# The quads' stages of a fused attention and mixture-of-experts kernel: behind a part's sums instead of between its products and its sums

## The chip, the cores and the metric

The kernel runs on one core of a Trainium2 chip. The metric is the device time of one execution in microseconds. The kernel before took 918.22 us, the median of three runs (918.18 to 922.17).

## The reference

For each of 4 batches, q, k and v have 3648 rows of 256 columns. The attention is over columns: q and k are normalised along the rows, a 256 x 256 matrix of their products goes through a softmax, and v is multiplied by it. The 14592 resulting rows x are then routed to 16 experts (4 groups of 4), each with two weight matrices:

```
s = kn.T @ qn / tau;  a = softmax(s);  x = v @ a
group = argmax(x @ w_group);  expert = argmax(x @ w_expert[group])
h = relu(x @ w1[group, expert])          # 256 -> 1024
out = gate weights * (h @ w2[group, expert])   # 1024 -> 256
```

## The kernel before

**Order of the whole.** The first third computes the attention, routes every row and scatters the rows into a buffer sorted by expert. Then the experts' work runs in three grains: 28 *items* of 512 rows of one expert each, 6 *quads* (128 rows, four pieces of 32 rows, each piece of an expert of its own), and up to 20 blocks of 128 rows behind the last item. The change touches the loop over the items, into which the quads are woven. From there on the program order on all five engines is written by hand.

**An item.** The loop runs over `seq`, 28 items times 8 parts (`f` = 0 to 7). One turn `n` does, for item `i` and part `f`:

- `ffn1(items[i], f)` (line 947): the part's *products*. Six matmuls of 512 columns give 128 of the 1024 hidden columns, in float32r pieces: w1 high with x high, w1 high with x low, w1 low with x high. ScalarE writes the high part of the Relu (`hh`, line 956), VectorE the low part (`hl`, line 957).
- The preparation of the next item: at f = 0 and 2 a half of its w1 is split into a high and a low part (lines 743 and 744, ScalarE and VectorE), at f = 5 and 6 a half of w2; at f = 3 and 4 its rows are turned and split.
- `ffn2(..., f - 2)` (lines 976 and 977): the *sums* of the part two turns back (`lag = 2`). For each of four groups of 128 rows, one matmul of 512 columns (`hh` with w2 high and low side by side) and one of 256 columns (`hl` with w2 high) add into that group's accumulator.
- After the sums of part 7, `finish` (line 1019): four times ScalarE scales one half of an accumulator into `ys` (line 993), VectorE adds the other half (line 994), and POOL scatters the rows (line 1005). `finish` of an item falls into part 1 of the next.

The four accumulators are four PSUM tiles (tags `acw` and `acc`, line 970), two of each, and each item takes all four. The products' outputs rotate over three PSUM tiles (tag `mm`), which the stages below share.

**A quad stage.** The quads' work is cut into 14 stages. The list `at` (line 1207) says in which of the last 24 items (j = i - 4) a stage stands: j = 0, 1, 3, 5, 7, ... 21, 22, 23. A stage does half of the hidden columns of one quad (`q_ffn1`, line 1091: 128 x 32 weights, 512 columns, four column tiles side by side) and half of the sums of the quad before (`q_ffn2`, line 1104, 256 columns). The first stage pair does only the former, the last only the latter. The stage's matmuls run at f = 2; its Relu goes to ScalarE (line 1094). VectorE transposes: the new quad's rows in 16 instructions (line 1076, `q_xT`), eight at f = 7 of the item before and eight at f = 0, for j = 0, 3, 7, 11, 15 and 19, where a quad begins; and the hidden rows at f = 3 to 6 (`q_hT`). `q_put` scales and scatters a finished quad at f = 3.

**Loads.** SP issues the weight loads and the 16 small copies that turn an item's rows (line 710). The quads' weights come through lines 1068 and 1071 into a single large tile (`qraw`, for one of the four pieces), two smaller ones (`qw`) and a ring (`qr`).

Of the kernel before, what the change touches and what calls it, by code (L numbers as in the profile page):

```python
# [61 lines left out]
def attention_moe(ctx: ExitStack, tc, q, k, v, tau, w_group, w_expert, w1, w2, out):  # L62
# [21 lines left out]
    def ring(*shape, name):  # L84
        return rp.tile([P, *shape], F32, tag="ring", name=name, bufs=RING)
# [602 lines left out]
    def fetch_x(d, tb, i):  # L688

        if d is items[0]:  # L690
            d["xg"] = raw_tile()[:, 0:4 * RW].rearrange("p (t w) -> p t w", t=4)
        else:
            d["xg"] = ring(4, RW, name="xg")
        d["nv"] = tb[1][:, i:i + 1]
        if tb is not tb_pre:
            gather(d["xg"].rearrange("p t w -> p (t w)"), tb[2][:, i:i + 1], 4)
            pause()
            return
        s = SP.value_load(tb[0][0:1, i, 1:2], min_val=0, max_val=DUMMY)
        ins = SP.dma_start(d["xg"].bitcast(I32), xs_d[ds(s, BIG), :].rearrange("(p t) w -> p t w", t=4))  # L700
        early.append(ins.ins)
        for o in late:
            tc.declare_no_dep(ins.ins, o, reason="the first items' slots have been filled")

    def quads_of(d):

        d["xq"] = ring(16, C // 4, name="xq")
        for q in range(4):
            for s in range(4):
                SP.dma_start(d["xq"][q * 32:(q + 1) * 32, s::4, :],  # L710
                             d["xg"][s * 32:(s + 1) * 32, :, q * 64:(q + 1) * 64])
# [160 lines left out]
    def where(i):  # L872
        return (items[i], tb_pre, i) if i < KPRE else (items[i], tb_big, i - KPRE)
# [114 lines left out]
    def put(d, t, src, on):  # L988
        ys = d["ys"]
        wcol = d["wc"][:, t:t + 1]  # L990
        if len(d["acc"]) == 4:
            a = d["acc"][t]
            ACT.activation(ys[:, t, :], a[:, 1, :], AF.Copy, scale=wcol)
            DVE.scalar_tensor_tensor(ys[:, t, :], a[:, 0, :], wcol, ys[:, t, :], ALU.mult, ALU.add)  # L994
        elif on == 0:
            ACT.activation(ys[:, t, :], src, AF.Copy, scale=wcol)
        else:
            DVE.tensor_scalar(ys[:, t, :], src, wcol, None, ALU.mult)
        if any(d is o for o in items[0:2]):
            held.append((d, t))  # L1000
        else:
            send(d, t)
# [16 lines left out]
    def finish(d):  # L1019
        d["ys"] = ring(4, C, name="ys")  # L1020
        for t in range(4):
            put(d, t, None if len(d["acc"]) == 4 else d["acc"][t // 2][:, t % 2, :], t // 2 if "xT" in d else 0)

    def fetch_big(i, which):
        d, tb, k = where(i)
        fetch_w(d, tb, k, which)
# [16 lines left out]
    def q_rows(q):  # L1043
        gather(qs["xg"][q % 2], tb_pc[2][:, q:q + 1], 1)
        pause()

    def q_stage(s):

        q, hf = divmod(s, 2)
        return ([(0, q, hf)] if q < NQ else []) + ([(1, q - 1, hf)] if q else [])  # L1050

    def q_weights(s, ps_):

        fetched = qs.setdefault(s, {})
        for p in ps_:
            w = wp.tile([P, 2048], F32, tag="wraw2", name="qraw", bufs=1) if p == 0 else None
            for second, q, hf in q_stage(s):
                e = SP.value_load(tb_pc[0][0:1, 4 * q + p, 0:1], min_val=0, max_val=E - 1)
                if p == 0:
                    t = w[:, second * 1024:(second + 1) * 1024]  # L1060
                elif p == 1:
                    t = rp.tile([P, 1024], F32, tag="L", name="qw", bufs=2)
                else:
                    t = ring(1024, name="qr")
                fs = slice(hf * 512, (hf + 1) * 512)
                if second:
                    fetched[1, p] = t = t.rearrange("p (f d) -> p f d", d=C)
                    SP.dma_start(t, w2e[ds(e, 1), fs, :].rearrange("o (c p) f -> p (o c) f", p=P))
                else:
                    fetched[0, p] = t = t.rearrange("p (c f) -> p c f", c=2)  # L1070
                    SP.dma_start(t, w1e[ds(e, 1), :, fs].rearrange("o (c p) f -> p (o c) f", p=P))
# [133 lines left out]
    host = lambda i: i - UN0 if 0 <= i - UN0 < 4 * NQ else None  # L1205
    LAST = 4 * NQ
    at = [0] + [2 * s - 1 for s in range(1, 2 * NQ)] + [LAST - 2, LAST - 1]
    stage = lambda j: at.index(j) if j in at else None
# [9 lines left out]
    seq = [(i, f) for i in range(NBIG) for f in range(8)]  # L1218
# [35 lines left out]
    for n in range(len(seq) + lag):  # L1254
        if n == 8 * KPRE:
            pt_.close()
            wide.append(ctx.enter_context(tc.tile_pool(name="pw", bufs=2, space=PSUM)))
        if n < len(seq):
            i, f = seq[n]
            j, jn = host(i), host(i + 1)  # L1260
            if f == 3:
                if KPRE < i + 2 < NBIG:
                    fetch_x(*where(i + 2))
            if jn is not None and f == 5 and i + 2 < NBIG:
                fetch_big(i + 2, "w1")
            for now_, to in ((j, plan), (jn, plan_n)):
                for s_, p_ in to.get((now_, f), ()):
                    q_weights(s_, p_)
            if f == 7 and KPRE < i + 2 < NBIG:
                quads_of(items[i + 2])  # L1270
            if j is not None and f == 1 and i + 1 < NBIG:
                fetch_big(i + 1, "w2")
            if first(j) is not None and f == 1:
                q = first(j)
                tokens(qs["ids"][q % 2], qs["xg"][q % 2][:, C:C + 1], slotq, tb_pc[1][:, q:q + 1])
            if i == NBIG - 1 and f == 4:
                POOL.drain()
                ns = nc.values_load(nsub[0:1, 0:1], min_val=0, max_val=NSUB)
                tc.mark_branch_hint_location("subs", engines=[ET.PE, ET.Pool, ET.DVE, ET.Activation, ET.SP])
            if first(jn) is not None and f == (1 if jn else 3):  # L1280
                q_rows(first(jn))
            ffn1(items[i], f)
            for h in side.get(n, ((), ()))[0]:
                h()
            if KPRE < i + 1 < NBIG:
                if f in (0, 2):
                    split_w(i + 1, "w1", f // 2)
                if f == 3:
                    turn_x(items[i + 1])
                if f == 4:  # L1290
                    split_x(items[i + 1])
                if f in (5, 6):
                    split_w(i + 1, "w2", f - 5)
            for q, a in ((jn, 0),) if f == 7 else ((j, 2),) if f == 0 else ():
                if first(q) is not None:
                    q_xT(first(q), a)
                    q_xT(first(q), a + 1)
            if j is not None:
                s_ = stage(j)
                for second, q, hf in q_stage(s_) if s_ is not None else ():  # L1300
                    if f == 2:
                        (q_ffn2 if second else q_ffn1)(s_)
                    if 3 <= f < 7 and not second:
                        q_hT(q, hf, f - 3)
                    if f == 3 and second and hf:
                        q_put(q)
        if lag <= n < len(seq):
            i, f = seq[n - lag]
            if i < NBIG - 1 or f < 8 - TAIL:
                ffn2(items[i], f)  # L1310
            if f == 7:
                finish(items[i])
        if n == len(seq) + lag - 2:
            sub_tiles()
        if n == len(seq) + lag - 1:

            d = items[NBIG - 1]
            d["ys"] = ring(4, C, name="ys")
            order = [(t, f) for t in range(4) for f in range(8 - TAIL, 8)]
            order.insert(TAIL, order.pop(TAIL - 1))  # L1320
            for t, f in order:
                sums(d, t, f)
                if f < 7:
                    continue
                a, w = d["acc"][t], d["wc"][:, t:t + 1]
                ACT.activation(d["ys"][:, t, :], a[:, 0, :], AF.Copy, scale=w)
                send(d, t)
        for h in side.get(n, ((), ()))[1]:
            h()
        scatter(NJ)  # L1330
        if n == 8 * (KPRE + 4):
            rgens.append(tables_sub())
        if n >= 8 * KPRE:
            advance(1)
# [85 lines left out]
```

## Time and profile before

| | before |
|---|---|
| median of three runs | 918.22 us |
| profiled execution | 924.53 us |
| its span | 922.6 us |
| TensorE busy (share of the span) | 907.9 us (98%) |
| VectorE, ScalarE, POOL busy | 716.1, 497.2, 390.0 us |
| granted TensorE clock, mean | 0.999 |
| DMA | 232 GB/s mean, 213.88 MB |

The busy time is that of one profiled execution, whose own time lies outside the range of the three runs. A busy TensorE is not TensorE at its peak: matmuls are pipelined and overlap in the timeline, so what it spends on one is read from start to start.

### The profile page before, as it was taken

Reading aid. Unit: us, or ns where it says so; the run is one execution under the profiler, and the core shown is the slowest. Engines: PE = TensorE matmul, PEld = TensorE weight load, DVE = VectorE, ACT = ScalarE, POOL = GpSimd, SP = SyncE. Lnnn points to the kernel's source line nnn. Section 1 sums busy time; section 2 is a strip of 40 time slices with the busy share of each in tenths; the row PEclk is TensorE's granted clock in tenths of the full one; section 3 lists DMA queues with packets and bytes.
Section 4 is the critical chain, followed back from the end, with each engine's and each line's share of the span. In section 5 each row is a group of like instructions: output and inputs, shape, how many; then the busy total and the mean of one; then the engine's idle time right before and its main releaser. Section 6 shows DMA issues by size and latency. Waiting matters only on the chain. (4 is left out here: it accounts for less than half of the span.)

```text
span 922.6 us, 16837 instructions
## 1 busy us (share of the span) xinstructions
PE 907.9 (98%) x5500; PEld 769.7 (83%) x5500; DVE 716.1 (78%) x1519; ACT 497.2 (54%) x831; POOL 390.0 (42%) x569
## 2 busy tenths in 40 slices
PE   9999999998999999999999999999999999999997
PEld 7899998998889987878787887878687878787887
DVE  6898998976999778878877767786677858785852
ACT  6789788676654445444545454445454444444432
POOL 0001887886588682322332334333433334323213
PEclk9999999999999999999999999999999999999999
DMA  9985868364854477777777777777776767777740
GB/s 301 359 290 187 310 226 297 129 212 163 297 168 155 146 270 249 251 244 248 254 248 246 248 251 256 251 236 234 241 229 222 246 225 229 229 239 247 244 159 36
DMA packets 159164, 213.88 MB, mean 232 GB/s; under 512 B 63107, under 2 KB 117643, under 8 KB 159072
## 3 DMA queue, kind: packets, MB, share of 16 engines
q1 hardware_dynamic: 144128, 168.23, 56.2%
q0 software_dynamic: 14944, 44.54, 12.9%
q8 instruction: 44, 0.72, 0.3%
q14 instruction: 48, 0.39, 0.1%
HBM read 170.33 MB, written 31.39 MB: 219 GB/s over the span
## 5 line engine op out<-in xcount | busy, mean ns | idle before, releaser
L947 PE MATMUL hmm<-xth,ww 128*128 128x512 f32 x888 | 314.7, 395 | 0.8 <-issue 0.8
L956 ACT ACTIVATE hh<-hmm 128x512 fp32r<-128x512 f32 x222 | 132.8, 599 | 333.6 <-PE hmm L947 306.9
L1005 POOL DMA_INDIRECT out<-ys,ids x112 | 126.0, 1125 | 365.8 <-DVE ys L994 338.8
L976 PE MATMUL wacc<-ww,hh 128*128 128x512 f32 x736 | 265.8, 394 | 0.0
L957 DVE SCALAR_TENSOR_TENSOR hl<-hmm,hh 128x512 fp32r<-128x512 f32 x222 | 152.2, 689 | 115.9 <-ACT hh L956 95.9
L977 PE MATMUL wacc<-ww,hl 128*128 128x256 f32 x736 | 206.4, 280 | 0.1
L947 PEld LDWEIGHTS hmm<-xth,ww 128*128 128x128 f32 x888 | 166.5, 188 | 39.9 <-issue 2.2
L947 PE MATMUL hmm<-xtl,ww 128*128 128x512 f32 x444 | 175.1, 394 | 0.3 <-issue 0.3
L976 PEld LDWEIGHTS wacc<-ww,hh 128*128 128x128 f32 x736 | 138.1, 188 | 36.5 <-issue 4.1
L465 POOL DMA_INDIRECT x_sorted<-xs,si x112 | 131.2, 1171 | 65.6 <-issue 33.9
L744 DVE TENSOR_TENSOR ww<-wraw,ww 128x1024 fp32r<-128x1024 f32 x112 | 136.9, 1222 | 24.8 <-ACT ww L743 21.1
L977 PEld LDWEIGHTS wacc<-ww,hl 128*128 128x128 f32 x736 | 139.3, 189 | 7.4 <-issue 0.2
L743 ACT ACTIVATE ww<-wraw 128x1024 fp32r<-128x1024 f32 x112 | 118.0, 1054 | 13.2 <-DMA wraw<-in_moe_w 13.0
L947 PEld LDWEIGHTS hmm<-xtl,ww 128*128 128x128 f32 x444 | 83.7, 189 | 10.2
L159 POOL MEMSET zero<- 128x256 f32 x260 | 86.5, 333 | 0.3
L341 PE MATMUL xmm<-ahi,vth 128*128 128x276 f32 (+1 forms) x232 | 69.3, 303 | 1.1 <-ACT xs L344 0.8
L232 PE MATMUL sacc<-qkraw 128*128 128x256 f32 (+1 forms) x280 | 69.0, 387 | 0.8 <-DMA qkraw<-in_k 0.8
L341 PE MATMUL xmm<-alo,vth 128*128 128x276 f32 (+1 forms) x232 | 67.2, 291 | 0.0
L341 PE MATMUL xmm<-ahi,vtl 128*128 128x276 f32 (+1 forms) x232 | 67.1, 290 | 0.0
L216 DVE TENSOR_TENSOR sqa<-sqa,sq 128x1024 f32<-128x1024 f32 (+3 forms) x46 | 59.8, 1312 | 6.6 <-ACT sq L207 5.2
L1076 DVE STREAM_TRANSPOSE qhT<-qh 32x128 f32<-32x128 f32 x192 | 57.6, 300 | 2.7
L232 PEld LDWEIGHTS sacc<-qkraw 128*128 128x128 f32 (+1 forms) x280 | 50.9, 193 | 7.9 <-issue 1.2
(283 smaller groups left out, 1433.4 us busy)
## 6 DMA issues: line engine op xcount, KB each, us to landing
wraw<-in_moe_w SPq DMA_DIRECT2D x55, 1024.0 KB
qr<-in_moe_w SPq DMA_DIRECT2D x48, 512.0 KB
vr<-in_v SPq DMA_DIRECT2D x28, 512.0 KB
qkraw<-in_q SPq DMA_DIRECT2D x26, 512.0 KB
qkraw<-in_k SPq DMA_DIRECT2D x26, 512.0 KB
qraw<-in_moe_w SPq DMA_DIRECT2D x24, 512.0 KB
qw<-in_moe_w SPq DMA_DIRECT2D x24, 512.0 KB
xq<-xg SPq DMA_DIRECT2D x368, 32.0 KB
```

The costliest lines, as they stand in the source:

```text
L159: POOL.memset(zero[:, 0:256], 0.0)
L232: PE.matmul(d["acc"][:, c, :], kt[:rows, 1, cs], qt[:rows, 0, :], start=d.pop("first", True) and c == 0, stop=(g == NG), skip_group_check= ...
L341: PE.matmul(mm[:rows, :NE], vt[:, c, j * P:j * P + rows], at[:, c, :], start=(n == 0), stop=(n == 5))
L465: ins = POOL.indirect_dma_start(out=xs_d, out_offset=bass.IndirectOffsetOnAxis(ap=si[:rows, j:j + 1], axis=0), in_=xs[:rows, t, 0:RW].bitc ...
L743: ACT.activation(h, r, AF.Copy)
L744: DVE.tensor_tensor(l, r, h, ALU.subtract)
L947: PE.matmul(mm, wt[:, c, fs], xt[:, c, :], start=(n == 0), stop=(n == 5))
L956: ACT.activation(hh, mm, AF.Relu)
L957: d["hl"] = DVE.scalar_tensor_tensor(hl, mm, 0.0, hh, ALU.max, ALU.subtract)
L976: PE.matmul(d["acc"][t].rearrange("p c n -> p (c n)"), hh[:, tsl], d["w2w"][:, f, :], start=(f == 0), stop=(f == 7), skip_group_check=True)
L977: PE.matmul(d["acc"][t][:, 0, :], hl[:, tsl], d["w2h"][:, f, :], start=False, stop=(f == 7), skip_group_check=True)
L1005: ins = POOL.indirect_dma_start(out=out, out_offset=bass.IndirectOffsetOnAxis(ap=d["ids"][:, t:t + 1], axis=0), in_=d["ys"][:, t, :], in_o ...
```

## The change

In the turn of f = 2 the stage's matmuls are issued behind the sums (`ffn2`, there of part 0) instead of between the products with their preparation and the sums. The transposes and `q_put` stay where they are.

```diff
@@ -1298,8 +1298,6 @@
             if j is not None:
                 s_ = stage(j)
                 for second, q, hf in q_stage(s_) if s_ is not None else ():
-                    if f == 2:
-                        (q_ffn2 if second else q_ffn1)(s_)
                     if 3 <= f < 7 and not second:
                         q_hT(q, hf, f - 3)
                     if f == 3 and second and hf:
@@ -1310,6 +1308,10 @@
                 ffn2(items[i], f)
             if f == 7:
                 finish(items[i])
+        if n < len(seq) and seq[n][1] == 2 and host(seq[n][0]) in at:
+            s_ = stage(host(seq[n][0]))
+            for second, q, hf in q_stage(s_):
+                (q_ffn2 if second else q_ffn1)(s_)
         if n == len(seq) + lag - 2:
             sub_tiles()
         if n == len(seq) + lag - 1:
```

## Rows read from the trace of the kernel before

In the timelines the columns are: start in us, length in us, engine, line, operation, out<-in with the shape, count, and in brackets idle time of the engine before it and what ended it.

**Rows 1.** Page, part 1: TensorE's busy time, share of the span, instructions.

```profile
PE   907.9 (98%) x5500; PEld 769.7 (83%) x5500; DVE 716.1 (78%) x1519; ACT 497.2 (54%) x831; POOL 390.0 (42%) x569
```

**Rows 2.** Timeline of TensorE, the stage of item j = 3.

```profile
408.80 0.39 PE L947 MATMUL hmm<-xth,ww 128*128 128x512 f32 x1
409.12 0.62 PE L1091 MATMUL qmm<-qraw,qxT 128*32 128x512 f32 x1
...
412.39 0.39 PE L1104 MATMUL qacc<-qr,qhT 128*32 128x256 f32 x2
412.70 0.50 PE L976 MATMUL wacc<-ww,hh 128*128 128x512 f32 x1
413.04 0.28 PE L977 MATMUL wacc<-ww,hl 128*128 128x256 f32 x1
```

**Rows 3.** Timeline of VectorE, the same item.

```profile
406.46 2.05 DVE L1076 STREAM_TRANSPOSE qxT<-qxg 32x64 f32<-32x64 f32 x8
...
409.06 0.68 DVE L957 SCALAR_TENSOR_TENSOR hl<-hmm,hh 128x512 fp32r<-128x512 f32 x1
409.66 1.65 DVE L994 SCALAR_TENSOR_TENSOR ys<-wacc,wc,ys 128x256 f32<-128x256 f32 x4
```

**Rows 4.** Timelines, j = 7, 11, 15, 19: ys on VectorE, the stage's first matmul.

```profile
505.85 0.62 PE L1091 MATMUL qmm<-qraw,qxT 128*32 128x512 f32 x1
506.38 1.65 DVE L994 SCALAR_TENSOR_TENSOR ys<-wacc,wc,ys 128x256 f32<-128x256 f32 x4
...
602.58 0.62 PE L1091 MATMUL qmm<-qraw,qxT 128*32 128x512 f32 x1
603.51 1.65 DVE L994 SCALAR_TENSOR_TENSOR ys<-wacc,wc,ys 128x256 f32<-128x256 f32 x4
...
701.46 0.62 PE L1091 MATMUL qmm<-qraw,qxT 128*32 128x512 f32 x1
702.00 1.65 DVE L994 SCALAR_TENSOR_TENSOR ys<-wacc,wc,ys 128x256 f32<-128x256 f32 x4
...
798.19 0.62 PE L1091 MATMUL qmm<-qraw,qxT 128*32 128x512 f32 x1
798.72 1.65 DVE L994 SCALAR_TENSOR_TENSOR ys<-wacc,wc,ys 128x256 f32<-128x256 f32 x4
```

**Rows 5.** Timelines, an item without a stage: ys; first sums; next products.

```profile
434.22 1.65 DVE L994 SCALAR_TENSOR_TENSOR ys<-wacc,wc,ys 128x256 f32<-128x256 f32 x4
...
435.05 0.39 PE L976 MATMUL wacc<-ww,hh 128*128 128x512 f32 x1
...
436.44 0.39 PE L947 MATMUL hmm<-xth,ww 128*128 128x512 f32 x1
```

**Rows 6.** Timelines of the attention: TensorE held by VectorE.

```profile
161.86 0.69 DVE L319 TENSOR_TENSOR vtl<-vtr,vth 128x512 fp32r<-128x512 f32 x1
...
162.60 0.66 PE L317 MATMUL vtr<-ident,vr 128*128 128x128 f32 x4 [1.63 <-DVE vtl L319]
```

**Rows 7.** Timelines, j = 5: ys on VectorE, the stage's first matmul.

```profile
455.95 1.65 DVE L994 SCALAR_TENSOR_TENSOR ys<-wacc,wc,ys 128x256 f32<-128x256 f32 x4
...
457.39 0.62 PE L1091 MATMUL qmm<-qraw,qxT 128*32 128x512 f32 x1
```

**Rows 8.** Timelines, j = 0: the last item's outputs on ScalarE; the stage.

```profile
336.38 1.63 ACT L996 ACTIVATE ys<-yacc,wc 128x256 f32<-128x256 f32 x4 [0.73 <-PE yacc L985]
...
337.84 0.89 PE L1091 MATMUL qmm<-qr,qxT 128*32 128x512 f32 x2
```

**Rows 9.** Timelines, j = 15: the stage's last matmul, then SP's load.

```profile
704.73 0.39 PE L1104 MATMUL qacc<-qr,qhT 128*32 128x256 f32 x2
...
706.91 0.38 SPq L1071 DMA_DIRECT2D qraw<-in_moe_w  x1
```

**Rows 10.** Windows: stretch, length, busy of PE, PEld, DVE, ACT, POOL, granted clock, DMA share, GB/s.

```profile
655.00:659.00 4.00, 2.84 (x11) 1.59 (x11) 0.00 (x0) 0.00 (x0) 2.69 (x5) 1.00 0.40 119
```

## The prediction

> **What bounds the kernel now.** The page comes first: TensorE is busy for 907.9 us of the 922.6 us span [rows 1], so all its idle time together is 14.7 us, and every microsecond in which it has to stand in the items' part lengthens the run. The chain of waits names only the last scatters and does not help. Next is the timeline of TensorE around one quad stage, the one of the eighth item (j = 3) [rows 2]. The last product matmul of a part starts at 408.80 and a 512-column matmul takes 0.23 us, so it has streamed by 409.03; the stage starts at 409.12 (0.09 us lost). The stage's last matmuls start at 412.39 and follow each other every 0.21 us, so they end at 412.60; the sums start at 412.70 (0.10 lost), and their second matmul comes 0.34 us after the first where 0.23 is usual (0.11 lost: the first weight load is not covered). A stage thus costs 0.30 us at its two borders, and between them it runs without a gap. The reader is to see that TensorE waits for no data here: entry and exit look alike in the stages that I read.
>
> Third, the timeline of VectorE at the same place [rows 3]. It is late. It turns the quads' rows (eight transposes from 406.46), writes the rest of part 1's hidden rows at 409.06, and only from 409.66 on adds up the four outputs of the item before (ys, four of them in 1.65 us). These four instructions empty the four accumulators which the new item's first sums overwrite. All four are in use by each item, so the sums cannot go round them. In the kernel before, the stage's 3.58 us (409.12 to 412.70) lie between and cover this.
>
> **The change, part by part.** Only TensorE's order changes: eight sum matmuls of part 0 go in front of a stage's matmuls, 14 times. ScalarE's, VectorE's, POOL's and SP's instructions keep their order, since the sums of part 0 issue nothing on them and the stage issues only one Relu on ScalarE, which follows the same weight copy and precedes the same Relu as before. No matmul, transfer or instruction is added.
>
> *Five waits appear.* A stage whose quad is new (j = 3, 7, 11, 15, 19; j = 0 below) shares its item with 16 transposes, which make VectorE late. After the change the sums want accumulator t at S + 0.35 t, where S is 0.09 us before the old start of the stage, since the drain at entry falls away, and 0.35 us is a quarter of the 1.39 us that a part's sums take (435.05 to 436.44 [rows 5]). For j = 3, S is 409.03, and unhindered sums would end at 409.03 + 1.39 = 410.42. The last accumulator is free at 409.66 + 1.65 = 411.31; a matmul that waits for VectorE starts about 0.05 us after its release (161.86 + 0.69 = 162.55 against 162.60 [rows 6]). So the last pair starts at 411.36 and the sums end at 411.71: 1.29 us late. The first is held until 409.66 + 0.48 + 0.05 = 410.19 and would reach 411.70 with an uncovered load of 0.11, so both ways agree. For the others the same subtraction is (start of ys minus old start of the stage) + 0.75, from [rows 4]: 0.53 + 0.75 = 1.28, 0.93 + 0.75 = 1.68, 0.54 + 0.75 = 1.29 and 0.53 + 0.75 = 1.28. Sum: **+6.8 us**. Bounds: if j = 11 is late only as the others are, 6.4; if each of the four accumulators shows 0.11 us of uncovered load, 0.33 more in a stage, 8.5. I take 6.8, by the rows of the stages themselves.
>
> Queued behind the waiting sums on TensorE are the stage, then the products of part 3 and all that follows, so the delay is passed on in full. VectorE and ScalarE get slack from it, but nothing later on TensorE waits for them, so nothing is given back.
>
> *Other stages: no wait.* In j = 1, 5, 9, 13, 17, 21, 22, 23 VectorE has no transposes ahead of it: at j = 5, ys runs from 455.95 to 457.60, and the stage began at 457.39 [rows 7]. The sums would start at 457.30 and want their last accumulator at 458.35. Items without a stage are already in this order and show what is tolerated: ys ended at 435.87, 0.82 us after the sums had begun at 435.05, and they took 1.39 us without a gap [rows 5].
>
> *Stage 0 (j = 0).* Its item follows one whose outputs ScalarE writes; these end at 336.38 + 1.63 = 338.01 [rows 8], and the sums, from 337.68 on, use two new accumulators first and the two freed ones from 338.38. No wait. Here a gain is possible: the fourth column's matmuls came 0.27 us late (the pair at 337.84 takes 0.89 us, where one alone takes 0.62 [rows 2]), most likely for a weight tile still on its way. 1.39 us later that is gone: **-0.3 us**, between 0 and -0.3.
>
> *The borders.* There are still 14 entries and 14 exits. Entry now follows a 256-column matmul and exit leads into products instead of sums. No row shows these two pairs, so I bound them by the 0.30 us of [rows 2]: from all of it vanishing (14 x 0.30 = -4.2 us) to another 0.11 us, one uncovered load, at each stage (+1.5). I take 0: the matmul ahead of the drain has streamed in both cases, and the load behind it has the same 128 x 128 form.
>
> *SP.* The weights of a stage are freed 1.4 us later, plus the wait. The nearest next user is the load into the single quad buffer at 706.91 on SP, 2.0 us after the matmuls of j = 15 ended (704.73 + 0.21) [rows 9]; 1.39 + 1.29 would hold it 0.7 us. Behind it on SP stand the next weight loads, used more than an item (24 us) later. I take 0, and up to 1 us as an upper end. SP and POOL are passed by no moved instruction.
>
> Sum: 6.8 - 0.3 = +6.5 us. The profiled execution took 924.53 us, of which 922.6 are the span, and would become 931.0. It stood 6.3 us over the median of 918.22, part of it a stretch of 4 us at 655 in which TensorE was busy for only 2.84 with no data missing [rows 10], which I don't expect in most runs. On the median the sum is **924.7 us**, 0.7% slower.
>
> One rule of the Trainium skill speaks against the change more strongly than my sum. What the row shows: in that stretch at 655 TensorE stood in pieces for over a microsecond, and the granted clock stayed at 1.00, the 2.4 GHz level [rows 10]. "TensorE: Matmul & The Clock Gate", section "Part 1: The HAM clock gate", says that the throttled clock is the default and only activity lifts it, so an engine that stands can fall to half; by that rule the five waits would cost more than themselves (a rival below). The trace speaks for no fall.
>
> **Rivals.**
> 1. *VectorE isn't late in an undisturbed run.* If its transposes or its wait for ScalarE were a good microsecond shorter without the profiler, the last ys would end within 1.0 us of S and the sums would not wait. Place: the same five items. It decides if ys starts 1.25 us earlier against the stage than shown. For it: the eight other stages are that early. Against it: 16 transposes per new quad are work, and four of the five stages agree within 0.01 us. It gives 918.22 - 0.3 = 917.9 us, not slower.
> 2. *The borders cost less.* If the drain at entry or the uncovered load at exit goes with the new neighbours, up to 4.2 us come back: 924.7 - 4.2 = 920.5 us, within 0.5% of before. With rival 1 as well it would be 913.7, faster. For it: 0.09, 0.10 and 0.11 us are there to be had 14 times. Against it: the switch between 32-column and 128-column tiles happens as often as before.
> 3. *The later release of weights reaches TensorE.* If SP's 0.7 us holds become late weight copies in the five items and these hold the products behind them, 5 x 0.7 = 3.5 us more: 928.2 us. Against it: an item of cover.
> 4. *The clock falls after the waits.* Were a stage's 3.58 us to run at half the clock five times, 5 x 3.6 = 18 us more: 942.7 us. Against it: [rows 10].
> 5. *The diff doesn't reorder TensorE.* The program order of all five engines is written by hand here, so I give it nothing of its own.
>
> **How the numbers follow.** Forecast (five waits, borders as now) 0.76; rival 1 0.10; rival 2 0.08, and both together 0.02; rival 3 0.03; rival 4 0.01. A measurement of this kernel can tell about 0.5%, 4.6 us, from no change, so slower means over 922.8. The forecast's own ends are 6.4 - 0.3 = 6.1, less 1.0 for borders 0.07 us cheaper each = 5.1, or 923.3, and 8.5 + 1.0 for SP = 9.5, or 927.7. Slower: 0.74 of the forecast + 0.04 = 0.78; within 0.5%: 0.02 of it + 0.10 + 0.08 - 0.01 for a gain over 0.5% = 0.19; faster: 0.03. The range reaches from 920.3, which takes in most of rival 2, to 927.7; rivals 1, 3, 4 and both together, 0.16, lie outside.
>
> **What would show it.** In the changed profile the sums of part 0 stand ahead of the stage, and at j = 3, 7, 11, 15, 19 TensorE's weight load of the sums waits for ys on VectorE: five gaps of 1.1 us ahead of the sums and small ones between them. At the other nine stages there is none, at stage 0 the 0.27 us lag is gone, and each stage keeps 0.30 us at its borders. I am wrong if those five gaps are missing or under 0.7 us, if the entry after the sums or the exit into the products differs by 0.1 us or more, if later waits for weight tiles or a granted clock below 1.00 appear, or if the run stays under 922.8 us with the gaps in place.

## The result and the profile after

| | before | after |
|---|---|---|
| median (seven runs each) | 918.18 us | 924.55 us |
| ratio, 95% interval | | 1.0082 (1.0065 to 1.0100) |
| profiled execution | 924.53 us | 924.55 us |
| its span | 922.6 us | 922.7 us |
| TensorE busy | 907.9 us | 907.5 us |
| granted TensorE clock, mean | 0.999 | 1.00 |

The changed kernel is slower by 0.82%, that is 7.5 us (6.0 to 9.2); the two medians lie 6.4 us apart. Of all executions in this document one, of 4518.69 us in the first experiment, counts as slow and enters no ratio. The two profiled spans agree all the same, and this is the first thing to understand: they differ in a part that the change does not touch. In two timelines of TensorE, the first products of item 0 in the kernel before and after, and the last matmul of each:

```profile
238.28 1.92 PE L937 MATMUL hmm<-xth,ww 128*128 128x512 f32 x7
...
917.14 0.28 PE L964 MATMUL wacc<-ww,hl 128*128 128x256 f32 x1
```

```profile
232.57 1.69 PE L937 MATMUL hmm<-xth,ww 128*128 128x512 f32 x6
...
917.31 0.28 PE L964 MATMUL wacc<-ww,hl 128*128 128x256 f32 x1
```

The attention happened to end 5.7 us earlier in the execution after. The items' stretch (start of the first products to end of the last sums) is 679.1 us before and 685.0 after, 5.9 more. The one before contains the stand at 655 [rows 10]. From the stage of j = 13, which starts at 650.84, to that of j = 15 at 701.46 [rows 4] it takes 50.62 us, where 48.46 is usual (457.39 to 505.85, [rows 7] and [rows 4]), so the stand cost 2.2 us. Undisturbed the stretch grew by some 8.0 us, which lies within the 6.0 to 9.2 of the runs.

Where the time went, in the waits of TensorE after (us in total, times, longest):

```profile
PE wacc L976 <- DVE ys L994: 5.2, 5, 1.5
```

Five waits, none of which existed before. One of them, j = 7, in the timelines of TensorE and VectorE after:

```profile
501.72 0.39 PE L947 MATMUL hmm<-xth,ww 128*128 128x512 f32 x1
503.04 0.50 PE L976 MATMUL wacc<-ww,hh 128*128 128x512 f32 x1 [0.93 <-DVE ys L994]
503.37 0.28 PE L977 MATMUL wacc<-ww,hl 128*128 128x256 f32 x1
...
504.55 0.28 PE L977 MATMUL wacc<-ww,hl 128*128 128x256 f32 x1
504.76 0.62 PE L1091 MATMUL qmm<-qraw,qxT 128*32 128x512 f32 x1
...
508.34 0.51 PE L947 MATMUL hmm<-xth,ww 128*128 128x512 f32 x1
508.69 0.40 PE L947 MATMUL hmm<-xtl,ww 128*128 128x512 f32 x1
```

```profile
502.51 1.65 DVE L994 SCALAR_TENSOR_TENSOR ys<-wacc,wc,ys 128x256 f32<-128x256 f32 x4
```

The bracket shows 0.93 us, but the loss is more than the bracket, which begins only after the modelled end of the matmul before. From the last product's start to the stage's first matmul it takes 504.76 - 501.72 = 3.04 us. Unhindered it would be 0.23 (the product) + 1.39 (the sums) + 0.09 (the entry) = 1.71, so the delay is 1.33 us. It is 1.32 at j = 11, 15 and 19, and 1.93 at j = 3, where VectorE was later still, because ScalarE stood for a weight load 0.50 us ahead of a copy that VectorE needs. Sum: 7.2 us. The last ys ended at 502.51 + 1.65 = 504.16; the last pair of sums started 0.12 us behind that, at 504.28, and took 0.39 us (its second matmul starts at 504.55 and takes 0.12).

At a stage without new transposes, j = 5, there is no wait, and entry takes the same as before: 454.97 - 454.76 = 0.21, of which 0.12 are the 256-column matmul. The exit above is 508.69 - 508.34 = 0.35 where 0.23 is usual, again as before. In the fourth column of stage 0 the lag is gone (0.62 instead of 0.89 us, [rows 8]). In the timelines, TensorE after, and then VectorE before, the transposes for this stage:

```profile
333.46 0.62 PE L1091 MATMUL qmm<-qr,qxT 128*32 128x512 f32 x2
...
454.76 0.28 PE L977 MATMUL wacc<-ww,hl 128*128 128x256 f32 x1
454.97 0.62 PE L1091 MATMUL qmm<-qraw,qxT 128*32 128x512 f32 x1
```

```profile
336.00 2.06 DVE L1076 STREAM_TRANSPOSE qxT<-qxg 32x64 f32<-32x64 f32 x8
```

One more term was not foreseen. Between two stages TensorE runs parts of the same 14 matmuls with no gap, yet not always at the same pace. In the timeline of TensorE before, the first product of a part, 15 parts apart, behind the stages of j = 3 and j = 5:

```profile
414.20 0.39 PE L947 MATMUL hmm<-xth,ww 128*128 128x512 f32 x1
...
455.90 0.39 PE L947 MATMUL hmm<-xth,ww 128*128 128x512 f32 x1
...
462.46 0.40 PE L947 MATMUL hmm<-xth,ww 128*128 128x512 f32 x1
...
504.36 0.40 PE L947 MATMUL hmm<-xth,ww 128*128 128x512 f32 x1
```

And after, 14 parts apart, behind j = 5:

```profile
461.44 0.40 PE L947 MATMUL hmm<-xth,ww 128*128 128x512 f32 x1
...
500.55 0.40 PE L947 MATMUL hmm<-xth,ww 128*128 128x512 f32 x1
```

A part takes 41.70 / 15 = 2.780 us in the first stretch and 41.90 / 15 = 2.793 in the second; after, 39.11 / 14 = 2.794. Before, the pace changed from one value to the other at each stage from j = 1 to j = 21, so 82 parts ran at 2.780. After, all of them run at 2.793. That makes 82 x 0.0135 = 1.1 us between these two executions. The account of the items' stretch is then 7.2 - 0.3 + 1.1 = 8.0 us, the 8.0 that were read.

### The profile page after: what moved, and what is told of

Same layout as the page of the kernel before. It is cut to its first block, busy times and chain, and to the rows that moved or that the text cites. A ratio compares the mean times of both kernels' runs of the same rounds, so it can differ in the third digit from the quotient of the medians.

```text
span 922.7 us, 16820 instructions
## 1 busy us (share of the span) xinstructions
PE 907.5 (98%) x5500; PEld 769.6 (83%) x5500; DVE 716.0 (78%) x1519; ACT 496.9 (54%) x831; POOL 391.6 (42%) x569
## 5 line engine op out<-in xcount | busy, mean ns | idle before, releaser
L465 POOL DMA_INDIRECT x_sorted<-xs,si x112 | 133.1, 1189 | 58.7 <-issue 26.4
```

What stands on the lines that cost most here:

```text
L465: ins = POOL.indirect_dma_start(out=xs_d, out_offset=bass.IndirectOffsetOnAxis(ap=si[:rows, j:j + 1], axis=0), in_=xs[:rows, t, 0:RW].bitc ...
```

## The experiments

Each ratio is to executions of the kernel before that were measured together with the run; their medians are 922.87 us for the first four experiments here, 917.7 for the doubled transposes and the cut stage, and 918.2 for the two with idle transposes. Times of different groups are not to be compared.

**Which stages lose the time.** The same two lines in each, with a condition on the stage: `behind(j)` is true for j = 3, 7, 11, 15, 19 in the first kernel and for the other nine in the second.

```diff
+    behind = lambda j: bool(j) and first(j) is not None
...
+                    if f == 2 and not behind(j):
+                        (q_ffn2 if second else q_ffn1)(s_)
...
-        if n < len(seq) and seq[n][1] == 2 and host(seq[n][0]) in at:
+        if n < len(seq) and seq[n][1] == 2 and host(seq[n][0]) in at and behind(host(seq[n][0])):
```

> Only the five stages in which a quad begins (j = 3, 7, 11, 15, 19) stand behind the sums, the other nine as before. Theory (the sums wait for the accumulators that VectorE empties late): all of the loss is here, five waits of 1.3 to 1.9 us, 6.5 to 7.5 us over the kernel before, ratio 1.007 to 1.008. Rival A (each border of a stage costs more with its new neighbours): 5/14 of the loss, some 2.5 us, ratio 1.003. Rival B (weights freed later are loaded later, and something waits for them): also about 5/14, with waits for weight loads in the trace.

Measured: ratio 1.0062 (1.0040 to 1.0084), that is 5.7 us (3.7 to 7.8), which excludes the 2.5 us of the two rivals. Its waits of TensorE:

```profile
PE wacc L976 <- DVE ys L994: 5.1, 6, 0.9
```

Five waits as in the changed kernel, here all of 0.9 us, that of j = 3 too, and a sixth of 0.5 us in the item behind j = 3, which has no stage: the same item was near its limit before [rows 5].

> The counterpart: the nine other stages (j = 0, 1, 5, 9, 13, 17, 21, 22, 23) stand behind the sums, the five as before. Theory: no wait, 0 to -0.3 us (stage 0's late column), ratio 1.000. Rival A and rival B: 9/14 of the loss, some 5 us, ratio 1.005.

Measured: ratio 1.0000 (0.9986 to 1.0014), and no wait for ys. The nine stages can stand on either side of the sums, the five cannot. With nine of fourteen stages at no cost, neither new neighbours nor later weights carry the loss.

**Taking VectorE's lateness away.** The transposes of a new quad's rows, for all quads but the first, move to the item before:

```diff
             for q, a in ((jn, 0),) if f == 7 else ((j, 2),) if f == 0 else ():
-                if first(q) is not None:
+                if first(q) == 0:
                     q_xT(first(q), a)
                     q_xT(first(q), a + 1)
+            for a in {5: (0,), 6: (1,), 7: (2, 3)}.get(f, ()):
+                if first(jn):
+                    q_xT(first(jn), a)
```

> The changed order, but the 16 transposes of a new quad's rows (all quads but the first) stand earlier on VectorE: four at f = 5, four at f = 6 and eight at f = 7 of the item before, which has no stage, and none at f = 0. Nothing else moves. Theory: VectorE is in time, ys ends about 0.3 us after the sums' start as in the items without a stage, the five waits are gone and the time is that of the kernel before, ratio 0.999 to 1.001. Rivals A and B: the loss stays, ratio 1.007 to 1.008.

Measured: ratio 1.0018 (1.0001 to 1.0034). Timelines of VectorE and TensorE at j = 7:

```profile
505.31 1.65 DVE L994 SCALAR_TENSOR_TENSOR ys<-wacc,wc,ys 128x256 f32<-128x256 f32 x4
```

```profile
506.66 0.39 PE L976 MATMUL wacc<-ww,hh 128*128 128x512 f32 x1
...
507.94 0.28 PE L977 MATMUL wacc<-ww,hl 128*128 128x256 f32 x1
508.15 0.62 PE L1091 MATMUL qmm<-qraw,qxT 128*32 128x512 f32 x1
```

ys starts 1.35 us ahead of the sums, ends 0.30 us into them, and the sums do not wait for it; of the five items only j = 3 still loses some 0.2 us to it. The order is the changed one and the loss is gone but for 0.2%, 1.7 us (0.1 to 3.1). Where that rest comes from is open. The slower pace, which all but one of its stretches keep, would give 0.9 us of it (67 parts x 0.0135). The profiled execution also has a wait of 0.7 us for `hl` behind a late weight load, as the kernel with the nine stages has (0.4 us), and one execution does not tell whether it comes often.

> The order of the kernel before with the same earlier transposes. Theory: VectorE's lateness was covered there, so its going brings nothing, ratio 1.000. If it is faster by 0.2% or more, VectorE's lateness cost something before too, by a way that I don't see.

Measured: ratio 0.9998 (0.9985 to 1.0010), as expected. VectorE's lateness cost nothing before that these runs could tell, 1.4 us at most.

**Making VectorE later.** The eight transposes of f = 0 are done twice in the five items:

```diff
                     q_xT(first(q), a)
                     q_xT(first(q), a + 1)
+                    if f == 0 and q:
+                        q_xT(first(q), a)
+                        q_xT(first(q), a + 1)
```

> The changed order, and the eight transposes at f = 0 of j = 3, 7, 11, 15, 19 are done twice (the same data again), 2.05 us more for VectorE in each of the five items. Theory: the sums wait 2.0 us longer in each, so 10 us more than the changed kernel, about 17.5 us over the kernel before, ratio 1.018 to 1.020. If the waits were for anything but VectorE, ratio 1.008 as the changed kernel.

Measured: ratio 1.0258 (1.0237 to 1.0279), 6 us more than expected. The waits grew as they should, four of them by 2.15 us. The rest is the clock. Timeline of TensorE at j = 3, and windows on both sides of it (length, busy of PE, PEld, DVE, ACT, POOL, granted clock, DMA share, GB/s):

```profile
406.82 0.60 PE L976 MATMUL wacc<-ww,hh 128*128 128x512 f32 x1 [3.40 <-DVE ys L994]
...
413.53 0.50 PE L947 MATMUL hmm<-xth,ww 128*128 128x512 f32 x1
```

```profile
403.00:407.00 4.00, 0.60 (x3) 0.18 (x2) 3.79 (x15) 1.54 (x2) 0.00 (x0) 1.00 0.23 49
407.00:410.80 3.80, 3.80 (x16) 2.14 (x20) 2.67 (x5) 0.00 (x0) 3.59 (x4) 0.55 0.50 118
```

Behind the wait the granted clock is 0.55 on average, which is mostly the 1.2 GHz level, and sums and stage take 413.53 - 406.82 = 6.71 us, where the changed kernel takes 508.34 - 503.04 = 5.30 at j = 7. This happened after four of the five waits, at about 1.5 us each: 6 us. By the Trainium skill's "TensorE: Matmul & The Clock Gate", section "Part 1: The HAM clock gate", a TensorE that stands idle for long enough falls back to the slow level. The trace agrees with that behind four of these five waits; behind the fifth, of 3.08 us at j = 15, the clock stayed at 1.00, as it did behind the waits of the change itself.

> The order of the kernel before with the same doubled transposes. Theory: the stage covers it. ys then ends 4.2 us after the stage's start, the sums start at 3.6 us and want their last accumulator at 4.6 us, so no wait but perhaps at j = 11: 0 to 0.5 us, ratio 1.000. If VectorE's work itself costs time, 10 us, ratio 1.011.

Measured: ratio 1.0100 (1.0076 to 1.0125), which is the other theory's number. The waits of TensorE show what I had overlooked; below them the transposes of VectorE and the stage's first matmul at j = 7:

```profile
PE qmm L1091 <- DVE qxT L1076: 3.2, 4, 0.8
PE qmm L1091 <- DMA xq<-xg: 1.8, 1, 1.8
```

```profile
502.57 4.28 DVE L1076 STREAM_TRANSPOSE qxT<-qxg 32x64 f32<-32x64 f32 x16
```

```profile
506.10 0.62 PE L1091 MATMUL qmm<-qraw,qxT 128*32 128x512 f32 x1 [0.79 <-DVE qxT L1076]
```

The stage reads the very rows that I had transposed twice, so it was the stage that waited, not the sums. It began when the first column's rows were ready and its other columns followed at the pace of the transposes. The wait of 1.8 us at j = 3 is put down to a load, but it is the same wait: there the stage starts 0.76 us before the transposes end (407.72 against 404.20 + 4.28), at j = 7 it is 0.75. With the slower columns the five stages lost 9.3 us in this execution, which accounts for the measured 1.0%. The experiment did not test the cover, so the next kernel delays ys by something that no one reads: eight transposes into the idle quad buffer at f = 1.

```diff
                 tokens(qs["ids"][q % 2], qs["xg"][q % 2][:, C:C + 1], slotq, tb_pc[1][:, q:q + 1])
+                for r in range(2) if q else ():
+                    q_turn(qs["xT"][(q + 1) % 2], qs["xg"][q % 2][:, r * C // 4:(r + 1) * C // 4].rearrange("p (k c) -> p c k", c=2), r)
```

> The order of the kernel before, and in the five items eight more transposes on VectorE at f = 1, ahead of the part's hidden rows and of ys, into the other quad buffer, which nobody reads: 2.05 us that delay ys alone and not the rows that the stage reads. Theory (the stage covers VectorE's lateness up to 3.58 us): ys ends 4.2 us after the stage's start and the sums want their last accumulator at 4.6, so 0 to 0.5 us, ratio 1.000. Rival (more work on VectorE costs TensorE time whatever the order, as the doubled transposes seemed to say): 9 us, ratio 1.010.

Measured: ratio 1.0011 (0.9995 to 1.0027). Timelines at j = 7, VectorE and then TensorE:

```profile
503.11 1.65 DVE L994 SCALAR_TENSOR_TENSOR ys<-wacc,wc,ys 128x256 f32<-128x256 f32 x4
```

```profile
500.54 0.62 PE L1091 MATMUL qmm<-qraw,qxT 128*32 128x512 f32 x1
...
504.12 0.50 PE L976 MATMUL wacc<-ww,hh 128*128 128x512 f32 x1
```

ys starts 2.57 us after the stage instead of 0.53, and the sums still start 3.58 us after it, at j = 15 and 19 too. At j = 3 and 11, where VectorE was later than that in this execution, they start 4.16 and 3.85 us after it: single columns of the stage waited for their rows, the sums then 0.12 us for ys, and these two items lost 0.7 and 0.4 us. So 2 us more of VectorE's work in each of five items cost 1.0 us in all in front of a covered instruction (no more than 2.5 by the interval), and 9 us in front of an uncovered one.

For the changed order the dose is halved: the same lines with `range(1)`, four transposes in each of the five items.

> The changed order with four such transposes, 1.03 us in each of the five items. Theory: each wait of the sums grows by 1.03 us to some 2.1 us, 5.2 us in all over the changed kernel, 12.7 us over the kernel before, ratio 1.013 to 1.014, with the granted clock at 1.00. If the clock falls after waits of this length as it did after those of 3.1 us and more, 5 x 1.5 = 7.5 us come on top, ratio 1.022.

Measured: ratio 1.0138 (1.0115 to 1.0160), with these waits:

```profile
PE wacc L976 <- DVE ys L994: 9.7, 5, 2.0
```

This is the ratio that the theory gave, 1.013 to 1.014. The waits grew from 5.2 to 9.7 us in the brackets, and by 1.01 us each from j = 7 on. The clock fell once, behind the first of them, and stayed at 1.00 behind the other four.

**The price of a border.** The stage is cut: `q_ffn1` in the old place, `q_ffn2` behind the sums.

```diff
+                    if f == 2 and not second:
+                        q_ffn1(s_)
...
-                (q_ffn2 if second else q_ffn1)(s_)
+                if second:
+                    q_ffn2(s_)
```

> The stage is cut: its first products (q_ffn1) stand in the old place, its sums (q_ffn2) behind the item's sums. In the ten stages that have both this adds one entry and one exit. Theory: the first half still covers VectorE's lateness (1.73 us and the exit against 1.3 us), so no waits, and the price of a border pair shows by itself: 10 x 0.30 = 3.0 us, ratio 1.003. If borders are free where no data is missing, ratio 1.000; if half a stage is too little cover, five waits come on top.

Measured: ratio 1.0023 (1.0010 to 1.0036), 2.1 us (0.9 to 3.3). Timeline of TensorE at the stage around 550:

```profile
550.70 0.60 PE L1091 MATMUL qmm<-qr,qxT 128*32 128x512 f32 x2
551.23 0.50 PE L976 MATMUL wacc<-ww,hh 128*128 128x512 f32 x1
551.57 0.28 PE L977 MATMUL wacc<-ww,hl 128*128 128x256 f32 x1
...
552.61 0.28 PE L977 MATMUL wacc<-ww,hl 128*128 128x256 f32 x1
552.82 0.40 PE L1104 MATMUL qacc<-qraw,qhT 128*32 128x256 f32 x1
```

The added exit loses 0.53 - 0.43 = 0.10 (550.70 to 551.23, where two such matmuls follow each other every 0.43) and 0.34 - 0.23 = 0.11 (551.23 to 551.57), the added entry 0.21 - 0.12 = 0.09: 0.30 us for the pair, ten times, 3.0 us in all, which the interval takes in. The sums wait nowhere, so half a stage was enough cover. The Trainium skill's "TensorEngine Tiling (Array Packing)", section "Key Properties", says that a change of the tiling mode drains the engine. The trace fits it, with 0.09 to 0.10 us lost at each switch; that a drain is what takes this time, no run shows.

## Why the prediction was right

The direction and the place were right, and the size nearly: +6.5 us was forecast, and the runs say 7.5 (6.0 to 9.2). That the median, 924.55 us, lies within 0.2 us of the forecast 924.7 is luck: the parts as the traces show them come to 8.0 us, 0.4 more from the waits and 1.1 from the pace, for which the sum had no term. By its own steps:

- *Five waits, +6.8 us.* They stand where they were forecast and nowhere else, on the instruction that was named. Four measured 1.32 to 1.33; for three of them 1.28 to 1.29 was forecast. At j = 7 the last pair of sums was 0.11 us slower than assumed (0.12 behind its release for 0.05, 0.39 for 0.35), and ys came 0.06 us sooner against the last product than before. The late one is a matter of the execution: j = 11 in the kernel before (1.68 forecast, 1.32 measured), j = 3 after (1.29 forecast, 1.93 measured), none where the five were moved alone. In sum 7.2 against 6.8; that each execution held one late item is luck too. That the loss lies in the sums' wait for VectorE was shown by moving the five stages alone, the nine alone, and the transposes, and by making ys later.
- *No wait at the nine other stages.* Right, ratio 1.0000.
- *Stage 0, -0.3 us.* The size was right and the cause wrong. I put the fourth column's lag down to a weight tile. In the trace before, the transposes for this stage run from 336.00 for 2.06 us, to 338.06, and the column started at 338.11: it waited for VectorE, as the stages of the doubled transposes did. The later place gave the rows time. But this gain too is a matter of the execution: in three runs with this stage in the old place (the five stages alone, the cut stage and the eight idle transposes) the rows were ready before the stage began, and no column came late.
- *The borders, 0.* Entry and exit keep 0.30 us, so the sum stands. But the two executions differ in something for which the forecast had no term: the pace of the parts behind a stage, 1.1 us in all. That the place sets it is not shown.
- *SP, 0.* No wait for weights appears on TensorE in either place.
- *The profiled execution, 931.0.* Wrong: 924.55 came. It was carried over from an execution of the kernel before whose attention ended 5.7 us later and which held the stand of 2.2 us at 655; neither belongs to the change. The median was the right base.
- *The rivals.* Rival 1 gave 917.9 us and fails on the time of all seven runs, 923.48 us at the least, and on the five waits. Rival 2 fails as put, since no border became cheaper. Rival 3 left no trace. Rival 4's mechanism exists, but it did not act here: the clock stayed at 1.00, and fell only in the kernels with longer waits, behind four of five of 3.1 to 3.4 us and one of five of about 2 us.

## What to carry to other kernels

A block of independent work in an engine's queue can be the cover for a slower engine, though the timeline shows no wait there; before it is moved, compare when the instruction behind it would start with when its operands and its output buffers become free, in each of the items and not only in a typical one. Of equal-looking stages five were late and nine were not, and the lateness came from what another engine did two parts earlier. If such a block must move, move the work that makes the other engine late as well: here that took the loss from 0.8% to 0.2%.

## What the runs showed of the hardware

- TensorE ran the same 14 matmuls, back to back, at two steady paces, 2.780 and 2.793 us, about 1 ns for a matmul. In the kernel before, nearly every stage switched between them; in the changed kernel the slower one was kept throughout. The order alone does not set it: in the two kernels of the changed order whose ys was made later, three stretches of 15 parts in each ran at the faster pace. What does is open.
- The granted clock fell to half, the 1.2 GHz level, after some waits of one length and not after others: four of five with brackets of 3.1 to 3.4 us, one of five at 1.9 to 2.0 us, and none of the changed kernel's five, up to 1.5 us. A fall cost about 1.5 us of slow matmuls.
- A wait that grows was therefore paid twice where it brought the clock down: in the changed order 2.15 us more of waiting cost 3.7 us at j = 7, while the fifth wait of the same length, at j = 15, left the clock up and cost its own 2.15.
